# A new plan for the same tasks: order, engines, buffer slots, and first-batch loads without holds

## The chip, the core and the metric

The kernel runs on one core of a Trainium2 chip. The core has five engines that run side by side, each through its own instruction queue, in program order: TensorE (PE in the profile; its weight loads are shown as PEld), VectorE (DVE), ScalarE (ACT), GpSimd (POOL) and SyncE (SP), which here issues transfers. Sixteen DMA engines move data between HBM and the on-chip memory. Engines wait for each other by semaphores. The metric is the device time of one execution, in microseconds (us).

## What is computed

Two layers, one after the other. The first is a linear attention with a decaying state, 4 batches, 8 heads, 768 steps, head size 48:

```python
for t in range(S):
    kt, vt, rt = (k[:, :, t], v[:, :, t], r[:, :, t])
    cur = np.einsum('bhd,bhe->bhde', u[None] * kt, vt)
    y[:, :, t] = np.einsum('bhd,bhde->bhe', rt, state + cur)
    state = w[None, :, :, None] * state + np.einsum('bhd,bhe->bhde', kt, vt)
```

The second is a mixer over its output x (4 x 768 x 384): a token layer and a channel layer.

```python
xt = x.transpose(0, 2, 1)
h = np.maximum(xt @ w_tok1, 0.0) @ w_tok2        # 768 -> 256 -> 768
u = x + h.transpose(0, 2, 1)
h2 = np.maximum(u @ w_ch1, 0.0) @ w_ch2          # 384 -> 1536 -> 384
return u + h2
```

Inputs and output are float32; the matmuls run in bf16.

## The kernel before the change

**Tiling.** The 768 steps of a batch are cut into six chunks of 128. For each chunk the kernel loads k and v (192 KB each; tiles kt and vt) and r. In batches 0 and 1 r comes in windows of two chunks (384 KB; tile win), in batches 2 and 3 by chunk (tile rt). Each chunk then goes through these steps:

- VectorE or GpSimd multiply k and r by powers of the decay (tile kr; in the profile `kr<-kt` and `kr<-win`); ScalarE or VectorE cast v to bf16 (vb).
- TensorE turns kr (trk for k, tr_ps for an r window; batches 2 and 3 turn most chunks by a DMA transpose); ScalarE or VectorE copy the result out (rka, rkb).
- TensorE makes the scores (at_ps), VectorE masks them (AT).
- The current step's own term goes through a product (pr), a small matmul (ad_ps), a copy (adg) and the "own" product with vb (yd, ydb).
- TensorE adds k times v to the state (kv_ps) and makes the output from state and scores (y_ps); it is copied to x_b.

When a batch has its six chunks, the mixer follows: the hidden token layer (h_ps from wtok; needs the weight part w0), the way back with w1 (hx_ps or hT_ps), then for each half of the batch 12 "up" groups of three matmuls (z_ps; w2 for the first four, w3 for the others), a relu on ScalarE or VectorE (zr), and 3 x 3 "down" groups of four matmuls (h_ps from wch; the thirds of wch2 are w4, w5, w6), the sum and the store. The attention of one batch is interleaved with the mixer of the batch before.

**Weights.** Seven transfers w0 to w6 bring the mixer's weights and turn them to bf16 on the way. They are issued by GpSimd, among its products. `W_DEP` (line 162) names for each a load that has to have landed before: w0 waits for v of batch 0, chunk 2; w1 and w2 for k of batch 0, chunk 5; w3 for v of batch 0, chunk 3; w4 to w6 for loads of batch 1.

**The plan.** All the work is a list of 910 tasks that `Plan.add` and `Plan.flex` (line 228) collect. `Plan.run` then emits them in the sequence of the list `ORDER`, written out as numbers. Each engine executes its own instructions in that sequence. `ENGINES` has one entry for each of the 307 tasks that can run on either of two engines. `BUFS` says for each buffer pool which slot the next tile takes; a tile waits until its slot's last reader is done. Twelve warm-up matmuls and a few filling ones (`FILL`) are part of the list.

**Loads.** `load` (line 499) issues from SyncE's queue. `HOLD` (line 163) makes thirteen loads of batch 0 and the first ones of batch 1 wait until an older load has landed; `GATES` (line 176) makes five later loads wait for a weight.

```python
            if (b, c, i) in GATES:
                after(asked[b, c, i], sent[GATES[b, c, i]])
            if (b, c, i) in HOLD:
                after(asked[b, c, i], asked[HOLD[b, c, i]])
```

Nearly every instruction passes through one helper, so the profile shows most of them on line 284, and groups are told apart by their tiles.

Of the kernel before, what the change touches and what calls it, by code (L numbers as in the profile page):

```python
# [1236 lines left out]
```

## Time and profile before

| | |
|---|---|
| time, three runs | 164.1, 166.72, 167.21 us; median 166.72 |
| the profiled execution | span 164.7 us, from its first to its last instruction |
| granted TensorE clock, mean | 0.99 |
| busy: TensorE / VectorE / GpSimd / ScalarE | 155.1 / 115.7 / 89.4 / 65.3 us |
| DMA moved | 26.35 MB, mean 160 GB/s |

The span of the profiled execution is the only time that goes with its rows; the page gives no time around it. "Busy" counts an engine's instructions, not its waits. The chain that ended last goes back from the last instruction to whatever released it, step by step. An idle engine costs time only where it stands on that chain.

### The profile page before, as it was taken

To read this page: it belongs to the slowest core of one execution; us is meant where nothing else is said; L and a number is where in the kernel's file an instruction comes from. 1 tells how busy PE (TensorE), PEld (TensorE's weight loads), DVE (VectorE), ACT (ScalarE), POOL (GpSimd) and SP (SyncE) were. 2 spreads that over 40 slices of the span, in tenths; PEclk is the share of its full clock that TensorE was granted. 3 is DMA by queue.
4 is the path that set the end of the run, shared out by engine and by line. 5 is a ranking of instruction groups with operands and counts; after the bars stand their busy time and mean duration, and the time that the engine had idled before them with its cause. 6 is when DMAs were issued, how large, how long until landed. Compare 5 with 4: busy or idle time off the path is not lost.

```text
span 164.7 us, 3813 instructions
## 1 busy us (share of the span) xinstructions
PE 155.1 (94%) x1474; PEld 103.8 (63%) x1475; DVE 115.7 (70%) x249; ACT 65.3 (40%) x145; POOL 89.4 (54%) x113
## 2 busy tenths in 40 slices
PE   6997799849999999999999999999999999999992
PEld 1464577525776777677676665677677656766661
DVE  6689894654986499689797968588989273763143
ACT  3989874504572452443407032136840200343000
POOL 7149990117482897999999998959722000000000
PEclk9999999986999999999999999999999999999999
DMA  4999899999989949999998997999640147310042
GB/s 128 196 205 182 142 241 217 208 212 213 206 147 232 174 94 192 233 232 182 187 235 172 202 180 135 209 210 204 138 119 4 48 90 188 113 44 0 0 185 102
DMA packets 90949, 26.35 MB, mean 160 GB/s; under 512 B 85683, under 2 KB 90037, under 8 KB 90933
## 3 DMA queue, kind: packets, MB, share of 16 engines
q1 hardware_dynamic: 88576, 22.88, 66.0%
q0 software_dynamic: 2160, 3.15, 11.2%
q8 instruction: 11, 0.18, 0.5%
q10 hardware_dynamic: 196, 0.11, 0.2%
q14 instruction: 6, 0.04, 0.1%
HBM read 20.46 MB, written 4.72 MB: 153 GB/s over the span
## 4 chain that ended last, share of the span: by engine, by line
PE 77%; DMA 17%; ACT 1%; SPq 1%; issue 1%; DVE 0%
PE h_ps L284 33%; PE z_ps L284 29%; DMA vt<-in_v_dram 12%; DMA kt<-in_k_dram 5%; PE y_ps L284 4%; PE hT_ps L284 3%; PE at_ps L284 3%; PE kv_ps L284 2%; PE tr_ps L284 1%; PE trk L284 1%; PE hx_ps L284 1%; ACT vb L284 1%; SPq L284 1%; ACT rkb L284 0%; PE ad_ps L284 0%
## 5 line engine op out<-in xcount | busy, mean ns | idle before, releaser
L284 PE MATMUL h_ps<-wch,zr 128*128 128x384 bf16 (+1 forms) x300 | 53.9, 320 | 0.0
L284 PE MATMUL z_ps<-uT,wch 128*128 128x384 bf16 x288 | 53.0, 334 | 0.7 <-ACT rka L284 0.7
L284 ACT ACTIVATE zr<-z_ps 128x384 bf16<-128x384 f32 x52 | 24.0, 492 | 48.3 <-PE z_ps L284 46.1
L284 PEld LDWEIGHTS <-wch 128*128 128x128 bf16 x288 | 31.9, 115 | 14.6 <-issue 1.5
L284 PEld LDWEIGHTS <-zr 128*128 128x128 bf16 x300 | 27.3, 98 | 15.1
L284 DVE TENSOR_TENSOR AT<-at_ps,mask 128x512 bf16<-128x512 f32 x48 | 30.6, 684 | 4.2 <-PE at_ps L284 3.9
L284 DVE TENSOR_SCALAR zr<-z_ps 128x384 bf16<-128x384 f32 x44 | 22.9, 551 | 9.0 <-PE z_ps L284 9.0
L284 POOL TENSOR_TENSOR yd<-vb,adg 128x384 f32<-128x384 bf16 x17 | 13.9, 827 | 15.3 <-DVE adg L284 7.3
L284 POOL TENSOR_TENSOR kr<-kt,wnat 128x384 bf16<-128x384 f32 x20 | 20.0, 1002 | 1.0 <-DMA kt<-in_k_dram 0.9
L284 PEld LDWEIGHTS <-kr 128*128 128x128 bf16 x192 | 12.9, 101 | 7.8 <-issue 2.6
L284 DVE TENSOR_TENSOR osb<-u_sb,h_ps 128x384 f32<-128x384 bf16 (+1 forms) x16 | 8.2, 526 | 10.1 <-PE h_ps L284 9.9
L284 DVE TENSOR_TENSOR x_b<-y_ps,yd 128x384 bf16<-128x384 f32 x18 | 9.5, 553 | 4.2 <-PE y_ps L284 4.0
L284 ACT CAST vb<-vt 128x384 bf16<-128x384 f32 x22 | 10.9, 512 | 3.3 <-DMA vt<-in_v_dram 3.1
L284 POOL TENSOR_TENSOR rku<-ku,rt 128x384 f32<-128x384 f32 x12 | 12.0, 999 | 0.2
L284 POOL TENSOR_TENSOR ku<-kt,u_bc 128x384 f32<-128x384 f32 x12 | 12.0, 1000 | 0.0
L284 POOL TENSOR_TENSOR kr<-rt,wp 128x384 bf16<-128x384 f32 x12 | 11.9, 996 | 0.0
L284 DVE TENSOR_TENSOR u_sb<-x_b,hT_ps 128x384 bf16<-128x384 bf16 x15 | 7.7, 550 | 4.5 <-PE hT_ps L284 4.4
L284 PEld LDWEIGHTS <-wtok 128*128 128x128 bf16 x78 | 7.4, 98 | 4.5
L284 POOL TENSOR_TENSOR pr<-rka,rkb 128x512 bf16<-128x512 bf16 x3 | 3.5, 1150 | 11.1 <-ACT rkb L284 7.4
L284 PE MATMUL kv_ps<-vb,kr 128*128 128x96 bf16 x80 | 6.7, 206 | 2.4 <-DVE vb L284 2.4
L284 PE MATMUL h_ps<-x_b,wtok 128*128 128x384 bf16 x48 | 8.8, 326 | 0.0
L284 PE MATMUL y_ps<-vb,AT 128*128 128x48 bf16 x192 | 8.7, 183 | 0.0
(96 smaller groups left out, 182.5 us busy)
## 6 DMA issues: line engine op xcount, KB each, us to landing
kt<-in_k_dram SPq DMA_DIRECT2D x24, 192.0 KB, 3.8
vt<-in_v_dram SPq DMA_DIRECT2D x24, 192.0 KB, 3.8
out_dram<-osb SPq DMA_DIRECT2D x23, 192.0 KB, 2.2
win<-in_r_dram SPq DMA_DIRECT2D x6, 384.0 KB, 5.6
rt<-in_r_dram SPq DMA_DIRECT2D x12, 192.0 KB, 4.2
wch<-in_moe_w_ch_dram POOLq DMA_DIRECT2D x4, 384.0 KB, 6.2
wtok<-in_moe_w_tok_dram POOLq DMA_DIRECT2D x2, 384.0 KB, 6.4
wch<-in_moe_w_ch_dram POOLq DMA_DIRECT2D x1, 768.0 KB, 11.1
```

The costliest lines, as they stand in the source:

```text
L284: return lambda *args, **kw: tc.keep_in_program_order(f(*args, **kw))
```

## The change

The tasks and their sizes stay. `ORDER`, `BUFS` and `ENGINES` get new contents, and `HOLD` becomes empty. `W_DEP`, `GATES`, `FILL` and all functions stay as they are. The number lists, cut to their first lines and to two pools:

```diff
 ORDER = [
-    0, 3, 22, 54, 18, 6, 16, 8, 898, 42, 59, 21, 899, 43, 39, 23, 53, 7, 13, 24, 19, 9, 2, 14, 56, 1, 11, 17, 4, 900,
-    20, 5, 10, 46, 901, 12, 25, 15, 64, 902, 30, 903, 29, 904, 162, 57, 31, 905, 126, 34, 906, 163, 61, 907, 32, 127,
...
+    3, 13, 59, 43, 1, 56, 0, 4, 15, 2, 907, 53, 46, 8, 22, 9, 39, 18, 11, 908, 20, 23, 21, 19, 42, 7, 58, 12, 901,
+    10, 14, 24, 54, 55, 63, 909, 25, 30, 906, 66, 32, 162, 5, 900, 61, 33, 126, 31, 902, 146, 57, 6, 130, 166, 35,
...
 BUFS = {
     'kt': [
-    0, 1, 2, 3, 4, 5, 0, 1, 2, 3, 4, 5, 0, 1, 2, 3, 4, 5, 0, 1, 2, 3, 5, 4,
+    0, 1, 2, 3, 4, 5, 0, 2, 1, 3, 4, 5, 0, 2, 1, 3, 4, 5, 0, 2, 1, 4, 0, 5,
...
     'vt': [
-    0, 1, 2, 3, 4, 5, 0, 1, 3, 2, 4, 5, 0, 3, 1, 2, 4, 5, 0, 3, 1, 2, 4, 5,
+    0, 1, 2, 3, 4, 5, 0, 1, 5, 3, 2, 4, 0, 1, 5, 3, 0, 4, 5, 1, 3, 4, 2, 0,
...
 ENGINES = [
-    0, 0, 1, 0, 1, 1, 1, 1, 1, 0, 1, 0, 1, 1, 1, 0, 0, 0, 1, 0, 1, 1, 1, 1, 0, 1, 1, 0, 0, 0, 1, 1, 0, 0, 0, 0, 0, 0,
...
+    1, 1, 1, 0, 0, 1, 1, 0, 1, 0, 0, 0, 1, 0, 0, 0, 0, 0, 1, 0, 0, 1, 0, 0, 0, 1, 1, 1, 1, 1, 1, 1, 0, 1, 0, 0, 0,
...
-HOLD = {(0, 4, 1): (0, 2, 1),
-        (0, 1, 2): (0, 0, 0),
-        (0, 3, 0): (0, 1, 0),
-        (0, 2, 0): (0, 4, 1),
-        (0, 4, 0): (0, 1, 2),
-        (0, 0, 2): (0, 3, 0),
-        (0, 2, 2): (0, 2, 0),
-        (0, 3, 2): (0, 4, 0),
-        (0, 4, 2): (0, 0, 2),
-        (0, 5, 0): (0, 2, 2),
-        (0, 5, 2): (0, 3, 2),
-        (1, 0, 1): (0, 4, 2),
-        (1, 0, 0): (0, 5, 0)}
+HOLD = {}
```

Read out for SyncE's queue, the first 28 loads are, by batch.chunk (rw is an r window of two chunks, named by its first):

| | |
|---|---|
| before | rw0.0 rw0.2 k0.0 k0.1 rw0.4 v0.1 k0.3 k0.2 k0.4 v0.0 v0.2 v0.3 v0.4 k0.5 v0.5 rw1.0 k1.0 v1.0 rw1.2 k1.2 v1.1 v1.2 k1.1 rw1.4 k1.3 k1.5 v1.3 k1.4 |
| after | rw0.2 k0.1 k0.0 k0.2 rw0.0 v0.0 k0.4 k0.5 k0.3 v0.1 rw0.4 v0.3 v0.4 v0.5 v0.2 v1.0 rw1.0 k1.0 k1.1 rw1.2 k1.2 v1.1 rw1.4 k2.1 v1.2 v1.3 r2.1 k1.3 |

And GpSimd's queue after its constants, up to w6 (kr, pr, own as above; ku is a product of k for the own term of batch 2; the letter after kr says what is multiplied):

| | |
|---|---|
| before | wp; kr rw0.4, k0.3, k0.2, k0.4; wGm twice; **w0**; own 0.0, 0.2; kr k0.5; **w1**; own 0.3, 0.4; **w2**; **w3**; pr 1.0; own 1.0; kr rw1.2; **w4**; kr k1.2, rw1.4; **w5**; kr rw1.4; **w6** |
| after | kr rw0.0, k0.0, k0.4; wp; kr k0.5; pr 0.0; wGm; kr k0.3, rw0.4; own 0.0; kr rw0.4; **w0**; own 0.1; pr 0.4; kr rw1.0; own 0.3; kr k1.0; **w1**; **w2**; kr rw1.2 twice; **w3**; kr k1.2; pr 1.1; own 1.0; pr 1.2; kr k2.1; **w4**; kr rw1.4, r2.1; ku 2.1; kr rw1.4; **w5**; kr k1.3, k1.5; **w6** |

On TensorE the twelve warm-up matmuls, the turns and the scores of batch 0 change places; seven groups of batch 1 (its first k v product, turns, a score) move ahead of the first up group of batch 0; two up groups that stood ahead of that k v product now stand behind it.

More of the change, by code (lines that the diff above doesn't have):

```diff
@@ L63 @@
     'AT0': [
-    0, 1, 2, 0, 1, 0, 2, 1, 0, 2, 1, 0, 2, 1, 0, 1, 2, 1, 0, 2, 1, 0, 2, 0,
+    0, 1, 2, 1, 2, 0, 1, 2, 0, 1, 2, 0, 1, 2, 0, 2, 1, 0, 2, 1, 0, 2, 1, 2,
 ],
     'AT1': [
-    0, 1, 2, 0, 1, 0, 2, 1, 0, 2, 0, 1, 2, 1, 0, 1, 2, 1, 0, 1, 2, 0, 1, 2,
+    0, 1, 2, 1, 2, 0, 1, 2, 0, 2, 1, 0, 2, 1, 0, 2, 1, 0, 2, 1, 0, 2, 1, 0,
 ],
@@ L78 @@
     'adg': [
-    0, 1, 2, 3, 4, 1, 0, 2, 3, 4, 1, 0, 2, 3, 4, 1, 0, 3, 2, 1, 4, 0, 3, 1,
+    0, 1, 2, 3, 4, 0, 2, 1, 3, 4, 0, 2, 1, 3, 0, 4, 2, 1, 3, 4, 2, 0, 1, 2,
 ],
@@ L84 @@
     'kp': [
-    0, 1, 2, 3, 4, 5, 0, 1, 4, 2, 3, 0, 4, 5, 1, 2, 3, 0, 5, 1, 4, 3, 2, 0, 5, 1, 4, 3, 2, 0,
+    0, 1, 2, 3, 4, 5, 1, 0, 1, 3, 1, 2, 4, 0, 3, 5, 1, 2, 4, 0, 1, 5, 2, 4, 0, 3, 5, 1, 4, 2,
 ],
     'kt': [
-    0, 1, 2, 3, 4, 5, 0, 1, 2, 3, 4, 5, 0, 1, 2, 3, 4, 5, 0, 1, 2, 3, 5, 4,
+    0, 1, 2, 3, 4, 5, 0, 2, 1, 3, 4, 5, 0, 2, 1, 3, 4, 5, 0, 2, 1, 4, 0, 5,
 ],
     'ku': [
-    0, 1, 2, 0, 1, 0, 2, 1, 0, 1, 2, 0,
+    0, 1, 2, 0, 1, 2, 0, 2, 1, 2, 1, 0,
 ],
@@ L96 @@
     'm': [
[7 rows of a table removed]
[8 rows of a table added]
 ],
     'osb': [
-    0, 1, 2, 2, 1, 0, 2, 1, 2, 0, 1, 2, 0, 2, 0, 1, 0, 1, 2, 1, 0, 2, 1, 0, 2,
+    0, 1, 2, 0, 0, 2, 1, 2, 2, 1, 2, 0, 0, 2, 1, 0, 2, 1, 1, 0, 2, 1, 0, 2, 1,
 ],
     'pr': [
-    0, 1, 1, 0, 1, 0, 1, 0, 1, 0, 1, 0,
+    0, 1, 1, 0, 1, 0, 0, 1, 0, 1, 0, 1,
 ],
     'rk': [
-    0, 1, 2, 3, 1, 0, 3, 2, 1, 0, 2, 3,
+    0, 1, 2, 3, 0, 1, 3, 2, 0, 1, 3, 2,
 ],
     'rka': [
-    0, 1, 2, 0, 1, 2, 0, 1, 2, 0, 2, 1,
+    0, 1, 2, 0, 1, 2, 1, 2, 0, 2, 1, 0,
 ],
@@ L120 @@
     'rku': [
-    0, 1, 1, 0, 1, 0, 1, 0, 1, 0, 0, 1,
+    0, 1, 0, 1, 1, 1, 0, 1, 0, 1, 0, 0,
 ],
     'rt': [
-    0, 1, 2, 3, 4, 0, 1, 3, 2, 0, 4, 3,
+    0, 1, 2, 3, 4, 0, 1, 2, 0, 3, 1, 4,
 ],
     'uT': [
-    0, 1, 2, 3, 0, 1, 3, 2,
+    0, 1, 2, 3, 1, 0, 3, 2,
 ],
@@ L132 @@
     'vb': [
-    0, 1, 2, 3, 4, 0, 1, 3, 2, 4, 0, 1, 2, 3, 4, 0, 2, 4, 1, 3, 0, 2, 4, 1,
+    0, 1, 2, 3, 4, 0, 1, 2, 4, 3, 0, 1, 2, 4, 3, 1, 0, 2, 4, 0, 3, 2, 1, 4,
 ],
     'vt': [
-    0, 1, 2, 3, 4, 5, 0, 1, 3, 2, 4, 5, 0, 3, 1, 2, 4, 5, 0, 3, 1, 2, 4, 5,
+    0, 1, 2, 3, 4, 5, 0, 1, 5, 3, 2, 4, 0, 1, 5, 3, 0, 4, 5, 1, 3, 4, 2, 0,
 ],
@@ L141 @@
     'yd': [
-    0, 1, 2, 0, 1, 2, 0, 1, 2, 1, 2, 0, 1, 2, 0, 1, 2, 0,
+    0, 1, 2, 0, 1, 2, 1, 2, 0, 2, 1, 0, 2, 1, 0, 2, 0, 1,
 ],
@@ L147 @@
     'zr': [
-    0, 1, 2, 1, 0, 1, 2, 0,
+    0, 1, 2, 0, 1, 2, 0, 2,
 ],
```

107 rows, old and new, of tables (BUFS, ENGINES, ORDER) are left out of this document.

## The prediction

> **What bounds the kernel now.** I read the page first, then the chain that ended last in order of time, then busy time by stretches.
>
> ```profile
> span 164.7 us, 3813 instructions
> ...
> PE 155.1 (94%) x1474; PEld 103.8 (63%) x1475; DVE 115.7 (70%) x249; ACT 65.3 (40%) x145; POOL 89.4 (54%) x113
> ...
> PE 77%; DMA 17%; ACT 1%; SPq 1%; issue 1%; DVE 0%
> ```
> ```profile
> 22.38 12.55 DMA vt<-in_v_dram
> ...
> 35.36 0.33 PE kv_ps L284 x4
> ...
> 36.26 3.66 PE z_ps L284 x12
> ...
> 40.12 3.92 PE z_ps L284 x24
> ...
> 161.63 0.35 DVE osb L284
> ```
> ```profile
> 20.00:36.00 16.00, 12.38 (x164) 8.94 (x164) 9.70 (x21) 7.81 (x20) 6.01 (x8) 1.00 1.16 219
> 36.00:60.00 24.00, 24.00 (x228) 16.43 (x226) 17.45 (x39) 10.74 (x22) 14.60 (x17) 0.93 1.00 191
> 60.00:72.00 12.00, 12.00 (x160) 8.87 (x158) 9.74 (x19) 4.89 (x14) 10.85 (x13) 1.00 0.83 183
> 72.00:108.00 36.00, 36.00 (x359) 24.44 (x358) 29.16 (x57) 11.53 (x27) 35.43 (x40) 1.00 0.99 193
> 108.00:164.70 56.70, 53.60 (x420) 36.00 (x418) 33.70 (x67) 15.02 (x34) 9.85 (x11) 1.00 0.40 101
> ```
> (Columns of the last: stretch, its length, busy time of PE, PEld, DVE, ACT, POOL, granted clock, DMA share, GB/s.) The page says that TensorE is busy 94% of the span, and the chain says where that is decided: from 36.26 to 161.6 it consists of matmuls alone, and TensorE is busy in every microsecond of 36 to 108. Before 36 us the chain hangs on transfers, with the DMA share above 1 from 20 to 36. So the kernel has two parts: a start of 36 us, ruled by the order in which transfers land, and 125 us of matmuls. The matmuls are the same ones after the change. A new order can win or lose time only where TensorE runs dry: in the start, or where an input comes late to the dense part.
>
> The span is 164.7 us and the median of the runs shown 166.72; the sum below is a difference against this execution, and I add it to the median. The runs reach from 164.1 to 167.21, so about 2% is what a measurement of this kernel can tell from no change.
>
> **What each load costs.** The first waits of the chain give the rate at which loads land, SyncE's issues show what holds them, and the page gives the weights.
>
> ```profile
> 1.94 5.24 DMA kt<-in_k_dram
> ...
> 7.26 3.72 DMA vt<-in_v_dram
> ...
> 11.01 3.20 DMA kt<-in_k_dram
> ```
> ```profile
> 1.94 2.34 SPq L284 DMA_DIRECT2D kt<-in_k_dram  x2
> 6.16 0.37 SPq L284 DMA_DIRECT2D win<-in_r_dram  x1
> ```
> ```profile
> q1 hardware_dynamic: 88576, 22.88, 66.0%
> q0 software_dynamic: 2160, 3.15, 11.2%
> ```
> Count a 192 KB load as one unit and an r window as two. The first k load is unit 5 and lands at 7.18; a later k load is unit 12 (counted off the old order) and lands at 14.21. That is 1.0 us a unit, from a start of 2.2: landing = 2.2 + units. The weights are 3.15 MB written, eight parts of 393,216 bytes; 11.2% of 164.7 us is 18.4, so 2.3 us of all DMA engines for a part. Check: the v load that ends the start is unit 22, and five parts (w0 to w3, the last of double size) went beside it: 2.2 + 22 + 11.5 = 35.7, and it landed at 34.93. I subtract that 0.8 where weights are counted.
>
> **The holds (HOLD = {}).** Thirteen loads no longer wait for an older one to land. That is worth nothing by itself. The first four loads have no hold even now, and the row shows the third and fourth taking 2.34 us to issue against 0.37 for a free one: the queue itself stops SyncE once a few loads are in it, and loads land at one unit per microsecond with the holds. Bounds: at most 1.0 us gained, one unit; nothing lost, because the loads of the rows below 20 us land in their order of issue. I take 0, the fit's own value.
>
> **The new order of the loads.** SyncE now issues: r window of chunks 2-3, k of 1, 0, 2, r window of 0-1, v of 0, k of 4, 5, 3, v of 1, r window of 4-5, v of 3, 4, 5, 2. The window of chunk 0 ends unit 7, at 9.2 instead of about 4.2; the last load of batch 0 is v of chunk 2, unit 18, at 20.2. That load is the one for which w0 waits (W_DEP).
>
> ```profile
> 7.96 0.57 POOL L284 TENSOR_TENSOR wp<-wp 8x128 f32<-8x128 f32 x1 [3.67 <-DMA wp<-in_u_dram]
> ...
> 15.32 1.93 POOL L284 TENSOR_TENSOR wGm<-bm,wG 128x384 f32<-128x384 f32 x2
> 17.20 1.02 POOL L284 DMA_DIRECT2D wtok<-in_moe_w_tok_dram  x1
> ...
> 21.00 0.61 POOL L284 DMA_DIRECT2D wtok<-in_moe_w_tok_dram  x1
> ...
> 23.40 1.66 POOL L284 DMA_DIRECT2D wch<-in_moe_w_ch_dram  x2
> 32.42 1.14 POOL L284 TENSOR_TENSOR pr<-rka,rkb 128x512 bf16<-128x512 bf16 x1 [7.37 <-ACT rkb L284]
> ...
> 44.73 0.60 POOL L284 DMA_DIRECT2D wch<-in_moe_w_ch_dram  x1
> ```
> ```profile
> L284 POOL TENSOR_TENSOR yd<-vb,adg 128x384 f32<-128x384 bf16 x17 | 13.9, 827 | 15.3 <-DVE adg L284 7.3
> L284 POOL TENSOR_TENSOR kr<-kt,wnat 128x384 bf16<-128x384 f32 x20 | 20.0, 1002 | 1.0 <-DMA kt<-in_k_dram 0.9
> ...
> wtok<-in_moe_w_tok_dram POOLq DMA_DIRECT2D x2, 384.0 KB, 6.4
> wch<-in_moe_w_ch_dram POOLq DMA_DIRECT2D x4, 384.0 KB, 6.2
> wch<-in_moe_w_ch_dram POOLq DMA_DIRECT2D x1, 768.0 KB, 11.1
> ```
> **What follows for the weights.** GpSimd issues them in its own program order, so they stand behind its products. Ahead of w0 and after 9.2 us it now has seven kr products (7.0), one pr (1.14), one own product (0.83), the wp product (0.57) and one wGm product (1.0): 19.7, so the v load decides and w0 goes out at 20.2 against 17.20. Ahead of w1 stands the kr product of batch 1's k of chunk 0, unit 22 with w0 beside it: 2.2 + 22 + 2.3 = 26.5, product done at 27.5, w1 at 27.5 against 21.00, w2 at 28.1 against 23.40. w2 lands 6.2 us later by its group, or 8.1 by the row of its own use (issued 23.40, first z at 31.47, below): 34.3 to 36.2; I take 35.3, the middle, since w1 stands ahead of it as it does now.
>
> ```profile
> 31.47 1.14 PE L284 MATMUL z_ps<-uT,wch 128*128 128x384 bf16 x6 [0.68 <-ACT rka L284]
> 32.54 0.40 PE L284 MATMUL at_ps<-rkb,rka 64*128 64x128 bf16 x8
> 35.36 0.33 PE L284 MATMUL kv_ps<-vb,kr 128*128 128x96 bf16 x4 [2.42 <-DVE vb L284]
> 35.53 0.65 PE L284 MATMUL z_ps<-uT,wch 128*128 128x384 bf16 x3
> ```
> Against that stands what the old order loses here: two z groups at 31.47, then 2.42 us dry for v of batch 1's chunk 0, then the z stream at 35.53. In the new order that v load is the first of batch 1 (unit 19), so this wait goes; what is late next is w2. When the z stream starts, the new order has 0.24 us more matmul work behind it (two z groups fewer, seven small groups of batch 1 more, counted off the lists at 0.163 us for a 384-column matmul, from 3.92 / 24). Starting at 35.3 it is 0.5 us ahead.
>
> **The clock.** Right after the 2.42 us of idleness twelve z matmuls took 3.66 us, 0.305 each, where the next 24 took 0.163, with a granted clock of 0.93 in that stretch: a loss of 12 x 0.142 = 1.7 us. In the new order TensorE waits for w1 (27.5 + 6.4 = 33.9) with its batch-0 attention done near 30; a wait of this kind is at least as long as the old one, so I keep the loss: 0 (bounds: -1.7 if the clock stays, +1.7 if it falls twice). [...]
>
> **The later weights.** Here the new order has its bottleneck. GpSimd's queue behind w3 holds: four products of batch 1, then the k product of batch 2's chunk 1, w4, an r window product, the r product of batch 2's chunk 1, two more, and only then w5. Those loads of batch 2 come through SyncE in the 24th and 27th place: units 30 and 33, with five weight parts beside them, so 2.2 + 30 + 11.5 - 0.8 = 42.9 and 45.9. Then: k product 43.9, w4 44.5, window product 45.5, r product 46.9, two products 48.9, w5 at 48.9 against 44.73. It lands 6.3 us later (its group), at 55.2. TensorE wants it for the first second-third of a down projection.
>
> ```profile
> 55.13 0.81 PE L284 MATMUL h_ps<-wch,zr 128*128 128x384 bf16 x4
> ```
> That is the same task before the change, at 55.13, with 0.26 us more matmul work ahead of it than in the new order. So the new order is 55.2 + 0.1 + 0.26 - 55.13 = **0.4 us behind** there: the half microsecond won at 35 us is given back to this wait. w3 says the same: behind the second window of batch 1 it goes out near 31, takes 11.1 as now, lands at 42.1, and is wanted 4.2 us (5.9 with the slow clock) after 35.3, thus a wait of 0.9 to 2.6 us; of these the 1.7 are the clock's loss in either case. Bounds of this term: -0.5 (w5 in time) to +5.2 (below).
>
> **Engines and slots.** Of the tasks that may run on either engine, 106 change. By count GpSimd gains four kr products and three pr and loses three own products, with a memset more: 4.0 + 3.4 - 2.5 + 0.3 = 5.3 us; VectorE loses some 2 us, ScalarE gains 1. What hides it: GpSimd sat idle for 10.0 of the 16 us from 20 to 36 (busy 6.01), where it now works. If that cover were gone it would cost up to 5.3, because GpSimd is full from 72 to 108 (35.43 of 36). VectorE has 2.5 us more work ahead of batch 1's hidden layer than before, in 36 to 60 where 6.5 us are free: 0, at most +1.5. The slots (BUFS) move waits for free buffers; I take 0, within the bounds that follow. From 72 us on I cost the new order at 0, since TensorE is dense there now and the same work stands in its queue; bounds -1.0 to +2.0, from the 3.1 us that it is idle after 108 (53.60 of 56.70), most of it behind the last matmul.
>
> Sum: 0 + 0 + 0.4 + 0 = +0.4, so 165.1 for the execution and **167.1** for the median.
>
> **The rivals.**
> - The dry spot goes and nothing takes its place. w2 lands at its early bound, 34.3 or sooner (33.6 if the k load of batch 1 isn't slowed by w0), 2.2 us ahead of 35.8; the clock stays up, 1.7; w5 goes out before 44. Then -3.9: 162.8. For it: the 12.55 us of the v load are the longest wait of the chain. Against: GpSimd's order puts products before every weight.
> [...]
> - Slower: GpSimd's queue holds the weights. SyncE's loads move slowly while weights move:
> ```profile
> 23.95 3.15 SPq L284 DMA_DIRECT2D win<-in_r_dram  x1
> 27.15 4.28 SPq L284 DMA_DIRECT2D kt<-in_k_dram  x1
> 31.47 4.83 SPq L284 DMA_DIRECT2D vt<-in_v_dram  x2
> ```
> five units took 12.3 us to issue there, 2.5 each. If w4 (2.3) passes ahead of the r load and the 0.8 isn't there, that load lands at 49.0, the products behind it end at 52, and w5, with w6 close behind, takes 8.1: 60.1, which is +5.2 and 171.9. It decides (+3.3, 2%) once w5 lands after 58.2. [...]
> - The change does nothing that counts: the queue held the loads anyway and the dense part rules. That is 166.7.
>
> **Chances.** Forecast 0.40 and no effect 0.07 (both within 2%), clock alone 0.12 (within 2%), nothing in its place 0.13 (faster), GpSimd's queue 0.28 (slower). So faster 0.13, same 0.59, slower 0.28. The range leaves out the fast rival and the far end of the slow one: 163.3 to 171.9.
>
> **What would show it.** Window of chunk 0 landing near 9, not 4; w0 issued near 20, w1 near 27.5, w5 near 49; no wait of TensorE for v of batch 1, a wait for wch near 35 and again near 53 to 55; one stretch of z matmuls at 0.3 us. If w5 goes out before 45 and TensorE is dense from 35, I was wrong on GpSimd's queue; if TensorE waits after 72 us, on the cover; if SyncE's issues of the first loads all take 0.37 us, on the holds.

## The result, and the profile after

The changed kernel takes **172.84 us** (median of four runs, 172.35 to 173.13) against 166.78 (median) beside it; the ratio is 1.051, 95% interval 1.046 to 1.055. That is 5.7 us above the forecast of 167.1 and above its range. Measured again beside later experiments it took 171.04 (169.79 to 171.78), a ratio of 1.026 (1.017 to 1.035). Times of one kernel scatter by several us from execution to execution (the kernel before, beside a6_v02 below, from 163.62 to 172.42); the ratios leave out executions more than 1.5% above the fastest of their kernel, among them most of those of the kernel before, so that 1.051 is more than the 1.036 of the two medians. Where a verdict hangs on less than 2 us it is read from the traces.

The page and the chain of the changed kernel, in the order in which those of before were read:

```profile
span 170.6 us, 3799 instructions
...
PE 158.9 (93%) x1474; PEld 105.9 (62%) x1475; DVE 118.1 (69%) x237; ACT 65.2 (38%) x152; POOL 95.3 (56%) x118
...
PE 80%; DVE 8%; DMA 6%; SPq 2%; POOL 1%; issue 1%; DVEq 0%; POOLq 0%
```
```profile
4.32 5.03 DMA win<-in_r_dram
9.50 1.37 POOL kr L275
10.91 1.89 PE tr_ps L275 x16
...
62.08 1.81 DVE place L275 x2
63.90 1.05 DVE place L275 x2
```
```profile
20.00:36.00 16.00, 14.87 (x203) 10.25 (x203) 12.53 (x23) 11.08 (x28) 11.61 (x13) 1.00 1.14 199
36.00:60.00 24.00, 23.77 (x252) 17.36 (x252) 20.33 (x40) 11.09 (x27) 15.72 (x20) 1.00 1.10 202
60.00:72.00 12.00, 10.60 (x122) 6.86 (x120) 11.13 (x23) 1.47 (x4) 10.54 (x11) 1.00 0.46 95
72.00:108.00 36.00, 35.95 (x364) 24.56 (x362) 25.60 (x51) 17.02 (x40) 30.17 (x33) 1.00 1.02 188
108.00:170.60 62.60, 59.57 (x479) 39.78 (x476) 37.39 (x74) 16.70 (x39) 15.89 (x18) 0.99 0.45 107
```
DMA has fallen from 17% of the chain to 6%, and TensorE has risen from 77% to 80%: the transfers no longer decide the start, and yet the span is 5.9 us longer. TensorE is busy 3.8 us longer (158.9 against 155.1) with the same 1474 rows, and from 20 to 36 us it is busy 14.87 us where it was busy 12.38. More busy time for the same matmuls points to slower matmuls; the spacing of single ones, below, shows it. A second loss stands at 60 to 72 us, where TensorE, without a gap before, is now idle for 1.4 us.

**Where they are.** I call *lag* the start of a group less the time of all matmul work ahead of it in TensorE's queue at full rate (0.163 us for a 384-column matmul, from 24 in 3.92 us; 0.056 for a turn, read below; warm-up matmuls aren't counted). What TensorE loses by waiting or by a slow clock appears as a rise of the lag, whatever the order. The first row of the hidden layer of batch 0, before and after, then the first z group:

```profile
24.12 1.14 PE L284 MATMUL h_ps<-x_b,wtok 128*128 128x384 bf16 x6
```
```profile
32.11 1.14 PE L275 MATMUL h_ps<-x_b,wtok 128*128 128x384 bf16 x6
...
41.25 1.17 PE L275 MATMUL z_ps<-uT,wch 128*128 128x384 bf16 x6
```
With 11.30 us of work ahead before and 11.75 after, the lags are 12.8 and 20.4: the new order is 7.5 us behind when batch 0's attention ends. It then regains 3.7, since neither the wait for v of batch 1 nor the slow z groups come; it loses 1.8 at 62 to 66 us and 0.4 in small steps over the rest: 7.5 - 3.7 + 1.8 + 0.4 = 6.0 at the last matmuls, where the spans differ by 5.9.

**The first 7.5.** TensorE's rows before and after:

```profile
7.19 1.97 PE L284 MATMUL tr_ps<-ident,kr 128*128 128x128 bf16 x16
...
9.80 0.91 PE L284 MATMUL u_ps<-wp,ones 1*128 1x384 f32 x2
```
```profile
5.38 1.49 PE L275 MATMUL kv_ps<-warm 128*128 128x512 bf16 x3
10.91 1.89 PE L275 MATMUL tr_ps<-ident,kr 128*128 128x128 bf16 x16 [4.04 <-POOL kr L275]
...
18.40 1.64 PE L275 MATMUL u_ps<-wp,ones 1*128 1x384 f32 x2
...
22.85 0.63 PE L275 MATMUL trk<-ident,kr 128*128 128x128 bf16 x4
```
The first r window lands at 9.35 and GpSimd's product of it ends at 10.86, so TensorE stands still for 4.04 us behind its warm-up matmuls, and its turns start 3.7 us later. And then it runs slowly: u_ps takes 1.64 us where it took 0.91, four turns of a k chunk 0.63 where the full rate gives 0.39. The starts of single turns are 107 ns apart until 26.3 us and 56 ns after; before, the change to 56 came at 8.9 us. TensorE doesn't lose a full rate in this pause, for it hasn't had one yet: the starts of the warm-up matmuls ahead of it are 0.43 us apart (three take 1.49), where a1_warm, below, has 0.22 once it is at the full rate. In the kernel before, full rate came after 7.6 us of work with few gaps (1.26 to 8.9 us); here the pause breaks into that work after 5.3 us. The page's clock row doesn't show the half rate:

```profile
PEclk9999999999999999999999999999999999999998
```
(40 slices of 4.3 us, 9 for full.) A fall from full rate showed: in a4_first2, below, the granted clock reads 0.57 over 12 to 24 us, where half rate comes back behind a full one (12.88 to 22.4). In the changed kernel, whose start had not been at full rate, it reads 1.00 from 10.91 to 26.3 us, and half rate is read there from the length of a known matmul (u_ps, 1.64 us against 0.91).

**The 1.8 at 62 us.** VectorE, then the matmul that waits for it, then VectorE's same copies before the change:

```profile
61.88 0.17 DVE L275 MEMSET place<- 128x128 uint32 x1
62.08 2.88 DVE L275 COPY place<-ident 64x64 bf16<-64x64 bf16 x4
64.97 0.69 DVE L275 TENSOR_TENSOR AT<-at_ps,mask 128x512 bf16<-128x512 f32 x1
```
```profile
65.71 0.45 PE L275 MATMUL at_ps<-rkb,rka 64*128 64x128 bf16 x8 [1.40 <-DVE AT L275]
```
```profile
3.81 0.64 DVE L284 COPY place<-ident 64x64 bf16<-64x64 bf16 x4
```
The constant `place` serves a way of pairing chunks that this kernel doesn't use; nothing reads it. The new order has moved its five operations from 3.6 us into VectorE's dense stretch, where the masks of batch 1 stand behind them.

### The profile page after: what moved, and what is told of

It is laid out like the page before. It is cut to its first block, busy times and chain, and to the rows that moved or that the text cites. A ratio compares the mean times of both kernels' runs of the same rounds, so it can differ in the third digit from the quotient of the medians.

```text
span 170.6 us, 3799 instructions
## 1 busy us (share of the span) xinstructions
PE 158.9 (93%) x1474; PEld 105.9 (62%) x1475; DVE 118.1 (69%) x237; ACT 65.2 (38%) x152; POOL 95.3 (56%) x118
## 3 DMA queue, kind: packets, MB, share of 16 engines
q0 software_dynamic: 2160, 3.15, 10.9%
## 4 chain that ended last, share of the span: by engine, by line
PE 80%; DVE 8%; DMA 6%; SPq 2%; POOL 1%; issue 1%; DVEq 0%; POOLq 0%
PE h_ps L275 31%; PE z_ps L275 25%; PE at_ps L275 6%; PE y_ps L275 5%; DMA win<-in_r_dram 3%; DMA uT<-u_sb 3%; PE hT_ps L275 3%; PE kv_ps L275 3%; DVE AT L275 3%; PE tr_ps L275 2%; PE trk L275 2%; SPq L275 2%; DVE place L275 2%; PE hx_ps L275 2%; DVE ydb L275 1%; PE u_ps L275 1%
## 5 line engine op out<-in xcount | busy, mean ns | idle before, releaser
L275 PE MATMUL h_ps<-wch,zr 128*128 128x384 bf16 (+1 forms) x300 | 53.3, 319 | 0.0
L275 PE MATMUL z_ps<-uT,wch 128*128 128x384 bf16 x288 | 51.0, 327 | 0.1
L275 ACT ACTIVATE zr<-z_ps 128x384 bf16<-128x384 f32 x55 | 24.6, 497 | 34.5 <-PE z_ps L275 34.3
L275 PEld LDWEIGHTS <-zr 128*128 128x128 bf16 x300 | 27.3, 97 | 15.3
L275 DVE TENSOR_SCALAR zr<-z_ps 128x384 bf16<-128x384 f32 x41 | 21.4, 552 | 13.8 <-PE z_ps L275 13.8
L275 POOL TENSOR_TENSOR yd<-vb,adg 128x384 f32<-128x384 bf16 x15 | 12.3, 831 | 15.6 <-DVE x_b L275 9.1
L275 POOL TENSOR_TENSOR kr<-kt,wnat 128x384 bf16<-128x384 f32 x20 | 20.1, 1014 | 0.1
L275 PEld LDWEIGHTS <-kr 128*128 128x128 bf16 x192 | 14.0, 109 | 8.8 <-POOL kr L275 4.9
L275 ACT CAST vb<-vt 128x384 bf16<-128x384 f32 x23 | 11.6, 517 | 4.0 <-DMA vt<-in_v_dram 4.0
L275 POOL TENSOR_TENSOR kr<-win,wpair 128x384 bf16<-128x384 f32 x8 | 9.0, 1129 | 6.2 <-DMA win<-in_r_dram 6.2
L275 POOL TENSOR_TENSOR pr<-rka,rkb 128x512 bf16<-128x512 bf16 x6 | 7.1, 1184 | 9.5 <-DVE rka L275 6.3
L275 PE MATMUL tr_ps<-ident,kr 128*128 128x128 bf16 x64 | 5.6, 244 | 4.0 <-POOL kr L275 4.0
```

Source lines behind the costliest of these rows:

```text
L275: return lambda *args, **kw: tc.keep_in_program_order(f(*args, **kw))
```

## The experiments

The theories at the start: (1) the *clock*, held at half rate by the pause before 10.9 us; (2) the *late window* by itself; (3) *GpSimd's queue*, which issues the weights behind products that wait for the other engines; (4) `place`; (5) the holds. The lags and spans of all profiled executions, in us ("half rate until" is read from the rows of turns and dummies, to a few tenths; in a4_first2 and b2_late it is the end of a second stretch; a1_warm, b3_v10 and b6_order fall to half rate once more later. A name with b is a variant of the kernel before, with a of the changed one; where tasks move in `ORDER`, `BUFS` is rewritten so that every tile keeps its slot.):

| run | first turns | half rate until | lag: hidden, batch 0 | lag: output of batch 1, chunk 0 | lag: hidden, batch 1 | lag: last matmuls | span |
|---|---|---|---|---|---|---|---|
| before | 7.2 | 8.9 | 12.8 | 18.3 | 18.8 | 20.3 | 164.7 |
| after | 10.9 | 26.3 | 20.4 | 22.1 | 24.6 | 26.3 | 170.6 |
| after_r1 | 10.9 | 18.6 | 17.1 | 20.1 | 23.4 | 24.7 | 169.1 |
| after_r2 | 11.0 | 18.4 | 17.1 | 20.5 | 23.9 | 25.6 | 170.0 |
| a6_v02 | 10.9 | 13.7 | 15.4 | 17.2 | 19.9 | 22.1 | 166.4 |
| a6_r | 10.8 | 26.1 | 20.2 | 22.9 | 25.3 | 26.9 | 171.3 |
| a1_warm | 10.9 | 9.1 | 18.8 | 20.5 | 24.0 | 25.3 | 169.7 |
| a2_first | 7.6 | 17.6 | 16.3 | 18.4 | 21.2 | 22.6 | 167.0 |
| a3_place | 10.9 | 23.9 | 19.2 | 21.1 | 22.0 | 23.4 | 167.8 |
| a4_first2 | 7.3 | 22.4 | 17.9 | 20.8 | 23.3 | 24.7 | 169.0 |
| a5_three | 11.0 | 9.2 | 15.0 | 17.7 | 18.8 | 20.1 | 164.5 |
| a7_best | 8.4 | 10.1 | 15.1 | 17.2 | 19.9 | 21.3 | 165.6 |
| a9_w1 | 10.8 | 9.2 | 15.1 | 18.8 | 20.5 | 22.1 | 166.5 |
| b1_nohold | 7.4 | 9 | 12.5 | 18.8 | 19.4 | 20.8 | 165.3 |
| b2_late | 7.0 | 20.3 | 17.5 | 18.9 | 19.9 | 21.4 | 165.8 |
| b5_cold | 6.9 | 19.4 | 15.1 | 16.5 | 17.1 | 18.5 | 162.9 |
| b3_v10 | 7.2 | 9.6 | 13.3 | 22.1 | 23.2 | 24.7 | 169.1 |
| b4_fill | 7.4 | 8.2 | 13.1 | 17.0 | 17.6 | 19.0 | 163.4 |
| b6_order | 7.0 | 7.0 | 15.2 | 17.1 | 17.6 | 19.1 | 163.5 |
| b8_fills | 7.2 | 8.7 | 13.5 | 15.1 | 17.3 | 18.8 | 163.2 |

**The holds alone (b1_nohold).** The kernel before, with

```diff
-HOLD = {(0, 4, 1): (0, 2, 1),
...
+HOLD = {}
```


> The kernel before with its nine holds taken out and nothing else changed. My prediction priced the holds at nothing: the time stays within 1 us of 166.7 and the loads land within 1 us of where they did. If the holds protect the first loads from the later ones, the first window and the first k chunks land later and the time rises by 2 us or more; if they hold back loads that are needed, it falls by 1 us or more.

(There are thirteen holds, not nine.) Measured 165.71 us, ratio 0.995 (0.984 to 1.005). The prediction's zero stands.

**The clock, by dummies in the pause (a1_warm).** The changed kernel with

```diff
-NWARM = 12
+NWARM = 24
-    130, 166, 35, 903, 127, 64, 163,
+    130, 166, 35, 903, 910, 911, 912, 913, 914, 915, 916, 917, 918, 919, 920, 921, 127, 64, 163,
```


> The changed kernel with twelve more 512-wide dummy matmuls on TensorE between its last opening dummy (ends 6.87 us) and the transposes of the first r window (start 10.91 us); nothing else moves. Theory 1, the cold clock: in the changed kernel TensorE stands still for 4.0 us before 10.91 us and then runs every matmul at half rate until about 26 us; if that is the cause, the transposes take 55 ns each in place of 107, the first back matmul comes at 33 to 34.5 us in place of 37.66, and the time falls by 3 to 5 us to 168 to 170. Theory 2, the late window alone: TensorE still starts at 10.9 us and the passing of the data between the engines sets the pace, so the first back matmul stays at 36.5 us or later and the time is 172 to 173.5. Theory 3, GpSimd's queue (w0, w1 and w2 go out at 22.7, 32.1 and 32.7 us): they move by under 1 us and so does the time.

TensorE's first turns and its later wait, then GpSimd:

```profile
10.88 1.07 PE L277 MATMUL tr_ps<-ident,kr 128*128 128x128 bf16 x16 [0.27 <-POOL kr L277]
...
23.94 0.32 PE L277 MATMUL y_ps<-ydb,ident 128*128 128x384 bf16 x1 [2.65 <-POOL ydb L277]
```
```profile
22.00 1.02 POOL L277 DMA_DIRECT2D wtok<-in_moe_w_tok_dram  x1 [2.02 <-DMA vt<-in_v_dram]
```
The sixteen turns take 1.07 us in place of 1.89, and the turns of rw0.4 start at 20.4 in place of 26.1: theory 1 holds for 5.7 us at that point. But 4 of them are given back. w0 waits on GpSimd for v0.2 (landed 21.7), the own product behind it is late, TensorE waits 2.65 us, and its clock falls again from 26 to 29.5 (granted clock 0.86 over 24 to 36 us). Time 170.9, ratio 1.029 (1.022 to 1.036): a gain of 2 us at most of the 3 to 5 expected, and none against the later executions of the changed kernel (171.04; spans 169.1 and 170.0 against 169.7 here). So the full rate by itself buys nothing that shows. Two things limit w0 at nearly the same time: GpSimd's products, which wait for a slow TensorE (22.68 us in the changed kernel), and the landing of v0.2 (22.00 us here). The late load that the prediction named was real, and hidden behind the slow clock.

**The window earlier (a2_first, a4_first2).** The changed kernel with the load of rw0.0 (54) second; a4_first2 also moves VectorE's second half of that product (127):

```diff
-    3, 13, 59, 43, 1, 56,
+    3, 13, 59, 54, 43, 1, 56,
...
-    10, 14, 24, 54, 55, 63,
+    10, 14, 24, 55, 63,
```
```diff
-    902, 146, 57, 6, 130, 166, 35, 903, 127, 64, 163,
+    902, 127, 146, 57, 6, 130, 166, 35, 903, 64, 163,
```


> The changed kernel with the load of the first r window (rw0.0) second in SyncE's queue instead of tenth or so; all else in the changed order. It should land at 6.5 to 7 us in place of 9.35, and each k chunk up to 2 us later. Theory 2 (the late window): the first transposes start 2 to 2.5 us sooner, near 8.5 us, and the time falls by 2 to 2.5 us if only the start counts. Theory 1 (the clock): TensorE's pause shrinks from 4.0 to about 1.6 us, the half-rate stretch ends by 12 us, and the time falls by 4 to 6 us, to 167 to 169. Theory 3 (GpSimd's queue sets the early part whatever the window does): the time moves by under 1 us.

> The changed kernel with the first r window second in SyncE's queue, as in a2_first, and VectorE's second product of that window (L663, the part that TensorE waits for) moved ahead of the products of k chunks 1 and 2 in VectorE's queue. In a2_first the window landed at 6.4 us but the second half of the transposes still began near 10.8 us, because VectorE stood on k chunk 2 (landed 9.5). If that queue is what spoiled the earlier landing, the first transposes run from about 7.6 to 9.5 us, TensorE's pause is 1 us or less, the clock is full by 12 us, and the hidden layer of batch 0 starts at 26 to 27.5 us (28.1 in a2_first, 32.1 in the changed kernel). If the clock is not restored by a shorter pause, matmuls stay at 107 ns until about 18 us and the hidden layer stays near 28.

a2_first: 169.35 us (166.4 to 170.7), ratio 1.008 (0.993 to 1.024). The window landed at 6.4, four turns ran at 7.6, the others only at 10.6, because VectorE stood on k0.2 first. a4_first2, where that queue is mended, was no faster (170.84, ratio 1.018, 1.010 to 1.026). Its TensorE rows say why:

```profile
10.35 0.40 PE L277 MATMUL tr_ps<-ident,kr 128*128 128x128 bf16 x4 [1.38 <-DVE kr L277]
...
12.88 0.59 PE L277 MATMUL ud_ps<-ident_f,wp 8*128 8x8 f32 x2 [1.16 <-POOL wp L277]
...
16.85 1.64 PE L277 MATMUL u_ps<-wp,ones 1*128 1x384 f32 x2
```
The turns at 10.35, behind a gap of 1.38 us, run at full rate (0.40 for four). Behind the next gap, of 1.16 us, ud_ps is at half rate (0.59 us for two, where the two wd_ps ahead of the gap took 0.38), and so is u_ps (1.64); it lasts until 22.4. So an earlier window by itself isn't the cure; and in a5_three, below, the window stays late and most of the loss goes, so theory 2 falls as the main cause. Here half rate followed a gap of 1.16 us, as in the changed kernel it followed one of 4.04.

**`place` early (a3_place).**

```diff
-    12, 901, 10, 14, 24, 54, 55,
+    12, 901, 10, 14, 17, 24, 54, 55,
...
-    396, 85, 426, 17, 325, 88,
+    396, 85, 426, 325, 88,
```


> The changed kernel with VectorE's five operations that fill the constant place put back among the first constants (before 4 us); no matmul reads that constant in this kernel. If they are what stops TensorE at 64.3 to 65.7 us (they hold VectorE from 61.9 to 64.95 us, ahead of the mask of chunk 3 of batch 1), the time falls by 1.2 to 1.8 us, to 171.0 to 171.6, and nothing changes before 60 us. If that gap has another cause (the copies of batch 1 are late anyhow), the time stays within 0.5 us of 172.8.

The gap at 64 us is gone: the lag rises by 0.9 from the output of batch 1 to its hidden layer where it rose by 2.5. So `place` costs 1.6 us in the changed kernel, and 0.62 us of VectorE's idle time where it stood. Times 165.9 to 171.4: the scatter hides it.

**Three mends together (a5_three).** The dummies, `place` early, and v0.2 (60) two places up:

```diff
-    165, 168, 218, 904, 65, 131, 169,
+    165, 168, 218, 904, 60, 65, 131, 169,
...
-    148, 176, 40, 60, 48, 149,
+    148, 176, 40, 48, 149,
```


> The changed kernel with three mends: the twelve dummy matmuls of a1_warm, the constant place early as in a3_place, and the load of v0.2 two places earlier in SyncE's queue (18 us in place of 21.7), because in a1_warm w0 stood on GpSimd waiting for v0.2 until 22.0 us with the own products behind it, and TensorE waited 2.9 us for those. If these are the causes, the hidden layer of batch 0 starts at 28.5 to 30 us in place of 32.1 (30.55 in a1_warm), TensorE's gap near 64 us goes, and the time is 166.5 to 169. If the gain given back in a1_warm has another cause (GpSimd's own list of products is too long), the hidden layer stays at 30.5 us and the time at 169 to 170.

168.25 us, ratio 1.016 (1.004 to 1.028), the profiled execution 166.2. GpSimd's weights, and TensorE's wait:

```profile
20.06 1.02 POOL L277 DMA_DIRECT2D wtok<-in_moe_w_tok_dram  x1
...
26.75 0.60 POOL L277 DMA_DIRECT2D wtok<-in_moe_w_tok_dram  x1
27.35 0.75 POOL L277 DMA_DIRECT2D wch<-in_moe_w_ch_dram  x1
```
```profile
33.26 1.46 PE L277 MATMUL hx_ps<-wtok,h1r 128*128 128x384 bf16 x8 [1.04 <-DMA wtok<-in_moe_w_tok_dram]
```
With the clock held and v0.2 sooner, w0, w1 and w2 go out within 0.8 us of where the prediction had put them (20.2, 27.5, 28.1), the last lag is 20.1 against 20.3 before, and the span 164.5 against 164.7. In this execution the three mends together take back the whole 5.9 us. It is the fastest of ten; their median is still 1.0 us above that of the kernel before beside it (167.22).

**v0.2 alone, and repeats (a6_v02, a6_r, after_r1, after_r2).** The last edit by itself, then the same kernel once more, and the changed kernel twice with nothing edited.

> The changed kernel with only the load of v0.2 two places earlier in SyncE's queue. In a5_three it came together with the dummies. If v0.2 counts only once TensorE is at full rate (in the changed kernel w0 goes out at 22.7 us, behind GpSimd's own products, after v0.2 has landed at 20.3), the time and the hidden layer (32.1 us) move by less than 0.7 us. If v0.2 was late by itself, the hidden layer comes 1 to 2.5 us sooner.

> The changed kernel once more, with nothing edited. Its half-rate stretch ended at 26.3 us in the profile shown; in variants that differ from it only later than 15 us (a3_place, a6_v02) it ended at 23.9 and at 15.0. If the end is a matter of the single execution, it falls elsewhere this time, between 14 and 27 us, and the times spread over 166 to 173 us with it; a profile with an end near 15 us has the hidden layer near 27 us in place of 32.1. If it belongs to the program, it ends within 0.5 us of 26.3 again and the times stay at 172 to 173.5.

> The changed kernel a third time, one execution with its profile: the same two readings as for after_r1. An end of the half-rate stretch more than 1 us from that of the other executions says that it is a matter of the single execution.

> The variant a6_v02 (v0.2 two places earlier in SyncE's queue) once more. If the early end of its half-rate stretch (15.0 us) came from the edit, it ends at 15.0 again; if from chance, it ends anywhere between 14 and 27 us, and the hidden layer, at 27.1 us the first time, goes with it.

TensorE in after_r1, a6_v02 and a6_r, a fence each:

```profile
18.39 1.00 PE L275 MATMUL u_ps<-wp,ones 1*128 1x384 f32 x2
...
28.87 1.14 PE L275 MATMUL h_ps<-x_b,wtok 128*128 128x384 bf16 x6
```
```profile
16.38 0.91 PE L277 MATMUL u_ps<-wp,ones 1*128 1x384 f32 x2
...
27.14 1.14 PE L277 MATMUL h_ps<-x_b,wtok 128*128 128x384 bf16 x6
```
```profile
18.27 1.64 PE L277 MATMUL u_ps<-wp,ones 1*128 1x384 f32 x2
...
31.97 1.14 PE L277 MATMUL h_ps<-x_b,wtok 128*128 128x384 bf16 x6
```
a6_v02 and a6_r are one program. In one execution the full rate came at 13.7 us (the expectations have 15.0; but the two wd_ps at 13.83 take 0.39 us, against 0.59 at half rate in after_r1), in the other at 26.1; the hidden layer came 4.8 us and the end of the span 4.9 us later. In the changed kernel itself it came at 26.3, 18.6 and 18.4. So **the half-rate stretch belongs to the change, and its length to the single execution.** The two traces of the one program were taken on different chips, but its four executions on one chip already run from 166.6 to 173.5 us. What v0.2 alone is worth stays open (ratio 1.014, 0.988 to 1.041): three of these four, at 168.1 or less, lie below every execution of the changed kernel (169.8 to 173.1), the fourth and a6_r (173.0) don't. Together with a1_warm this suggests that the two limits hide each other: full rate with a late v0.2 gives a span of 169.7, a sooner v0.2 with a long half-rate stretch 171.3, with a short one 166.4. What sets the moment at which full rate comes was not settled; TensorE is busy nearly all the time in every case (from 12 to 24 us for 11.78 us in the changed kernel, 11.75 in after_r1, 11.76 in after_r2, 11.36 in a6_v02, 12.00 in a6_r).

**The same loss put into the kernel before (b2_late, b5_cold).** b2_late loads rw0.0 fifth; b5_cold takes out eight of the warm-up matmuls (900 to 907), so that TensorE pauses for 3.0 us while no data comes later than before.

```diff
-    0, 3, 22, 54, 18, 6, 16, 8,
+    0, 3, 22, 18, 6, 16, 8,
...
-    15, 64, 902, 30,
+    15, 64, 54, 902, 30,
```
```diff
-    1, 11, 17, 4, 900, 20, 5, 10, 46, 901, 12, 25, 15, 64, 902, 30, 903, 29, 904,
+    1, 11, 17, 4, 20, 5, 10, 46, 12, 25, 15, 64, 30, 29,
```


> The kernel before with one edit: the load of the first r window moved from first to fifth in SyncE's queue, so that it lands near 9.5 us in place of 4.6 (as in the changed kernel). Theory 1, the clock: TensorE pauses for 2 us or more behind its opening dummies, its matmuls stay at half rate (107 ns a transpose) well past 9 us, and the time rises by 3 to 7 us, to 169.5 to 173.5; the first up matmul slides from 31.5 to 35 us or later. Theory 2, the late window by itself: the rise is the delay of the first transposes, at most 2.5 to 3.5 us, and the clock is back within 3 or 4 us of the restart. My prediction's reading (early delays hide behind the weights, which go out no later): within 1 us of 166.7.

> The kernel before without eight of its ten opening dummy matmuls (those from 3.80 to 7.40 us); every load, wait and product stays. TensorE then stands still from 3.9 to 7.2 us, and no data comes later. Theory 1, the clock: the transposes and the narrow matmuls behind that pause stay at half rate (107 ns a transpose) for 10 us or more in place of 1.8, and the hidden layer of batch 0 starts at 26 to 29 us in place of 24.1; part of that is taken up by the wait for v1.0 near 33 us, so the time is 167 to 170. Theory 2 (only late data costs): the hidden layer stays within 0.7 us of 24.1 and the time within 0.7 us of the kernel before.

TensorE's first turns in b2_late, then its first turns in b5_cold and the product that needs v1.0:

```profile
7.01 0.39 PE L289 MATMUL tr_ps<-ident,kr 128*128 128x128 bf16 x4
10.96 1.46 PE L289 MATMUL tr_ps<-ident,kr 128*128 128x128 bf16 x12 [3.56 <-DVE kr L289]
```
```profile
6.90 0.61 PE L288 MATMUL tr_ps<-ident,kr 128*128 128x128 bf16 x4 [3.03 <-DVE kr L288]
...
35.17 0.34 PE L288 MATMUL kv_ps<-vb,kr 128*128 128x96 bf16 x4
```
In both, half rate lasts until 19 or 20 us, and the hidden layer of batch 0 lags by 4.7 us (b2_late) and 2.3 us (b5_cold) more than before. b2_late had just reached full rate (0.39 us for four turns) and lost it in the pause of 3.56 us; b5_cold, like the changed kernel, had never had it. So late data isn't needed: taking work out of the start is enough for the stretch. But the ends differ little: 168.63 us, ratio 1.016 (1.011 to 1.022), and 165.22, ratio 0.999 (0.990 to 1.008). The old order has cover for it: its TensorE waits 2.42 us for v1.0. Here w1 and w2 go out later (23.3 and 25.7 us in b5_cold, 25.7 and 28.1 in b2_late, in place of 21.0 and 23.4), and v1.0 lands at 29.6 and 28.1 us in place of 34.9. TensorE doesn't wait for it, and its z groups run at full rate (2.12 us for twelve in both). In b5_cold the last lag is 1.8 us *below* that of before.

**The dry spot of the kernel before (b4_fill, b6_order, b3_v10, b8_fills).** b4_fill puts thirteen fillings ahead of the k-v product that waits for v1.0, b6_order moves that product (348) behind five z groups, b3_v10 moves the load of v1.0 ahead of rw1.0 and k1.0, and b8_fills is b6_order with five fillings more.

```diff
-FILL = {138: 2, 154: 1, 159: 1, 190: 1}
+FILL = {138: 2, 154: 1, 159: 1, 190: 1, 348: 13}
```
```diff
-    281, 338, 341, 345, 348, 347, 283,
+    281, 338, 341, 345, 347, 283,
...
-    262, 343, 350, 349,
+    262, 343, 348, 350, 349,
```
```diff
-    192, 172, 183, 159, 69, 186,
+    192, 172, 183, 159, 70, 69, 186,
...
-    226, 209, 70, 194,
+    226, 209, 194,
```
```diff
-FILL = {138: 2, 154: 1, 159: 1, 190: 1}
+FILL = {138: 2, 154: 1, 159: 1, 190: 1, 179: 1, 195: 1, 210: 1, 215: 1, 226: 1}
```


> The kernel before with thirteen dummy matmuls of 384 columns ahead of the k-v product of chunk 0 of batch 1, in the 2.4 us from 32.9 to 35.4 us in which TensorE waits for v1.0; they write a bank that the product then overwrites. If the twelve z matmuls at half rate behind that wait (36.1 to 39.8 us, 1.7 us lost) come from the pause, they run at full rate and the time falls by 1.2 to 1.9 us, with the wait itself unchanged. If the dip has another cause (a budget of power, say, after a busy stretch), it stays or comes later, and the time stays within 0.5 us.

> The kernel before with the k-v product of chunk 0 of batch 1, which waits for v1.0 until 35.4 us, moved behind five z matmul groups in TensorE's queue (2.45 us of work that needs nothing but w2, landed 31.0). Loads and waits stay. If TensorE's wait of 2.4 us and the half-rate groups behind it (1.7 us) are the terms that the prediction took them for, both go, and the time falls by 2.5 to 4 us, to 160.5 to 163.5. If the z results then wait for VectorE and ScalarE, which copy them, the gain is 1 us or less.

> The kernel before with the load of v1.0 moved two places up in SyncE's queue, ahead of the second batch's first r window and k chunk. It should land near 26 us in place of 34.9. If the prediction's two terms of the kernel before are right (2.4 us of waiting for v1.0, then 1.7 us of matmuls at half rate that follow from that pause), TensorE runs through from 31 to 40 us and the time falls by 3 to 4.5 us, to 162 to 164. If the clock dip does not follow from the wait, only 2 to 2.5 us go. If the delayed window and k chunk take the place of the wait, the time stays within 1 us of 166.7.

> The kernel before with the product of b6_order moved behind five z groups, and five more dummy matmuls ahead of chunk 2 to 5's scores and outputs of batch 0 (19 to 25 us, where TensorE has gaps that add up to about 3 us). In the profile of b6_order matmuls fell to half rate again from about 24 to 28 us. If those gaps are what lets the clock fall, it stays full and the time is 162 to 165, below the kernel before in every comparison; if the dummies only lengthen TensorE's queue (0.9 us of them), the time is that of b6_order (163.5 to 167) or 0.5 us above.

The z groups of b4_fill behind the wait, twelve matmuls:

```profile
36.48 2.12 PE L289 MATMUL z_ps<-uT,wch 128*128 128x384 bf16 x12
```
2.12 us (3.80 in the kernel before by the same view): the dip comes from the pause. With wait and dip in place the lag rises by 5.5 us from the hidden layer to the output of batch 1, chunk 0; it rises by 3.9 in b4_fill, without the dip, and by 1.6 in b8_fills, without either. The 1.7 and 2.4 us that the prediction named for them were sized rightly: 1.6 and 2.3. (b6_order rises by 1.9, but there a second half-rate stretch made the hidden layer late, and v1.0 landed at 29.5, so that the wait goes by itself, as in b5_cold.) As times: b4_fill 165.83 (ratio 1.006, 0.998 to 1.013), b6_order 166.12 (0.993, 0.981 to 1.004), b8_fills 165.32 (0.999, 0.994 to 1.004). Their medians lie 1.5 to 1.9 us below those of before beside them (167.68, 167.57 and 166.88), but the ratios show no gain, and b6_order misses the 160.5 to 163.5 expected. The fastest executions of the kernel before (163.6 to 165.7 us) may be those in which the clock stays up by itself: beside the experiments 14 of 16 of them have a granted clock of 0.998 or more, and 56 of the 59 slower ones 0.99 or less. No trace of one was taken, so that is open. In b8_fills part of the gain is lost again further on: TensorE, now sooner, waits 1.49 us at 51.51 us for w5, landed 51.47. b3_v10 missed: VectorE, then TensorE,

```profile
35.66 0.56 DVE L289 TENSOR_TENSOR kr<-kt,wnat 128x384 bf16<-128x384 f32 x1 [6.23 <-DMA kt<-in_k_dram]
```
```profile
36.74 0.61 PE L289 MATMUL tr_ps<-ident,kr 128*128 128x128 bf16 x4 [6.25 <-DVE kr L289]
```
k1.0 now comes beside w1, w2 and w3 and costs 6.25 us in place of 2.4 (167.6 to 171.4 us).

**The rest (a7_best, a9_w1).** a7_best combines a5_three with the earlier window, both halves of VectorE's products ahead of the k chunks, and the dummies split; a9_w1 is a5_three with w1 (120) directly behind the first own product:

```diff
-    902, 146, 57, 6, 130, 166, 35, 903, 127, 64, 163, 202,
+    902, 163, 127, 146, 57, 6, 130, 166, 35, 903, 910, 911, 912, 913, 64, 202,
...
-    165, 168, 218, 904, 65,
+    165, 168, 218, 904, 914, 915, 916, 917, 918, 919, 920, 921, 60, 65,
```
```diff
-    201, 153, 158,
+    201, 153, 120, 158,
...
-    227, 51, 120, 79,
+    227, 51, 79,
```


> The changed kernel with the mends of a5_three, and the first r window second in SyncE's queue, VectorE's second halves of the first two windows ahead of its products of k chunks 1 and 2, and the twelve dummies split: four behind the opening ones and eight behind the first four groups of transposes. If the clock is the reason why the earlier window brought nothing in a4_first2, the transposes run at 8 to 10.5 us, all at full rate from about 9 us, the hidden layer of batch 0 starts at 24 to 26 us (26.8 in a5_three) and the time is 164 to 167. If GpSimd's list of products (13 us of them ahead of w0) binds in its place, the hidden layer stays at 26 to 27 us and the time at that of a5_three, 166 to 168.5.

> The mended kernel of a5_three with w1 also moved, from behind four of GpSimd's products (23.5 to 26.8 us) to behind the first own product after w0, so that it goes out near 22 us in place of 26.75. In a5_three TensorE waits 1.0 us for w1 (32.2 to 33.3 us; landed 33.2), in a6_r too (w1 landed 38.4). If GpSimd's list is what holds the weights at this point, that wait goes and the time falls by 0.7 to 1.2 us. If w1 going out sooner only takes the share of the transfers from k1.0, v1.0 or w0, TensorE waits as long for one of those, and the time stays within 0.5 us of a5_three.

a7_best: 168.15 us, ratio 1.019 (0.999 to 1.040). Turns at 8.4 and full rate from 10.1, and yet the hidden layer starts at 26.8 as in a5_three. GpSimd works without a gap from 11.6 us to w0 at 19.46, so its list is the likely limit; TensorE's waits there are short (0.95 us for VectorE, 0.59 for GpSimd), so this isn't shown. Further on TensorE waits 1.52 us at 42.30 us for w3, landed 42.26. a9_w1: 169.21, ratio 1.019 (1.009 to 1.028). The wait for w1 is gone; GpSimd and TensorE show what came instead:

```profile
28.85 0.99 POOL L277 TENSOR_TENSOR kr<-kt,wnat 128x384 bf16<-128x384 f32 x1 [2.93 <-DMA kt<-in_k_dram]
```
```profile
29.90 0.40 PE L277 MATMUL trk<-ident,kr 128*128 128x128 bf16 x4 [1.90 <-POOL kr L277]
```
Here w1 goes out at 21.62 us in place of 26.75, and GpSimd's product of k1.0 starts at 28.85, behind 2.93 us of waiting for that load, in place of 25.81: the wait moved from w1 to k1.0. No version beat the kernel before.

## Why the prediction was wrong

The prediction held that "a new order can win or lose time only where TensorE runs dry". That premise fails: up to 26.3 us the same matmuls ran at half rate (turns 107 ns apart in place of 56), and no term of the sum had a price for it.

- **The holds**: right, 0.
- **The new order of the loads**: right as landings (rw0.0 at 9.35, v0.2 at 20.3). With the clock held, v0.2 lands at 21.7 (a1_warm). Wrong in what followed: the 5 us by which the first window comes later were priced only through the weights. That TensorE pauses for 4 us there has no term, though the prediction itself priced what a pause does at the z groups.
- **What follows for the weights**: this is **the step that failed**. It added GpSimd's busy times ("19.7, so the v load decides and w0 goes out at 20.2") and took "batch-0 attention done near 30". GpSimd's products wait for copies of what TensorE made (2.20 and 1.60 us for adg in the rows below), so a slow TensorE slows them too, and TensorE in turn waits for them (2.65 us for ydb in a1_warm). GpSimd in the changed kernel:

```profile
20.95 0.83 POOL L275 TENSOR_TENSOR ydb<-vb,adg 128x384 bf16<-128x384 bf16 x1 [2.20 <-ACT adg L275]
...
22.68 1.02 POOL L275 DMA_DIRECT2D wtok<-in_moe_w_tok_dram  x1
25.31 0.82 POOL L275 TENSOR_TENSOR ydb<-vb,adg 128x384 bf16<-128x384 bf16 x1 [1.60 <-ACT adg L275]
...
32.09 0.61 POOL L275 DMA_DIRECT2D wtok<-in_moe_w_tok_dram  x1
32.69 0.76 POOL L275 DMA_DIRECT2D wch<-in_moe_w_ch_dram  x1
...
48.21 0.61 POOL L275 DMA_DIRECT2D wch<-in_moe_w_ch_dram  x1
```
w0 went out 2.5 us, w1 and w2 4.6 us after their forecast, and the z stream began at 41.25 in place of 35.3. The wait for v1.0 did go. In a5_three, where the clock is held and v0.2 is loaded sooner, the issues come near the forecast (20.06, 26.75, 27.35), the z stream 1.5 us late (36.84, behind a wait of 1.04 us for w1). With the clock held and v0.2 in its place (a1_warm), w0 goes out at 22.00 and z starts at 39.66: two terms of this step were too low, the products' waits and the landing of v0.2.
- **The clock**: the loss of 1.7 us that I kept at the z groups didn't come (twelve take 2.12 us at 42.35, where the kernel before took 3.80: the bound of -1.7, the "clock alone" of the chances, held there), and a larger one that I didn't look for came 25 us earlier. By the lags, the new order was to be 0.5 us ahead when the z stream starts and is 3.8 us behind amid it, a miss of 4.3.
- **The later weights**: w5 went out at 48.2 (forecast 48.9) and landed at 53.8, and TensorE, late itself, didn't wait for it. The 0.9 us of this wait, from 0.5 ahead to 0.4 behind, didn't come. That late weights can hold TensorE up isn't refuted: where it is sooner it does wait, for w3 in a7_best (1.52 us) and, in the kernel before, for w5 in b8_fills (1.49 us).
- **Engines and slots**: mis-sized. VectorE ahead of batch 1's hidden layer was 0, at most +1.5; it measured 1.8, of which `place` is 1.6. I had counted tasks whose engine changes, not constants that merely change their place.
- **The rivals**: GpSimd's queue did hold weights, but w0 to w2, not w5, and as the carrier of TensorE's lateness; the price named for it (171.9) came near by another way, which is luck. That the dry spot goes and nothing takes its place was half true: it went.

The sum of the misses: 4.3 - 0.9 + 1.8 + 0.4 (the small steps) = 5.6, and 0.4 + 5.6 = 6.0 at the last matmuls.
